# Decay attention and a two-layer MoE block on one core: low halves of all weights on VectorE, two more jobs in float32, decay rows by products, smaller first groups, and a planner with other costs

## The chip, the core and the metric

The kernel runs on one core of a Trainium2 chip. The core has five engines that run side by side, each in its own fixed order: TensorE (PE) for products, VectorE (DVE), ScalarE (ACT) and GpSimd (POOL) for element work, and SyncE (SP), whose queue issues all transfers. They wait for one another by semaphores. The metric is device time in microseconds (us); one execution was also recorded by the hardware profiler.

## What is computed

Eight batches of eight heads with 576 rows and 64 columns each: attention with a decay, then a feed-forward block over the 4608 rows of 512 columns that result.

```python
scores = scale * np.matmul(q, k.transpose(0, 1, 3, 2))
cum = np.cumsum(np.log(np.clip(f, 0.0001, 1.0)), axis=-1)
decay = cum[:, :, :, None] - cum[:, :, None, :]
scores = np.where(causal, -1000000000.0, scores + decay)
attn = softmax(scores)
x = np.matmul(attn, v)                  # to (4608, 512)
h = x @ w_in                            # (4608, 2048)
g = where(h >= 1, h, where(h <= -1, 0, (h + 1) ** 2 / 4))
out = g @ w_out                         # (4608, 512)
```

All inputs are float32. The kernel gets float32 accuracy from float16 products by splitting each factor into a high half and a low half (the rest), and adding three products: high by high, low by high, high by low. A product in float32 is the other way: one product, which PE takes in several passes.

## The kernel before

**Jobs.** Attention is cut into 36 jobs of two heads each (`jobs`). The first batch is cut in rows: jobs one to four do rows 0 to 255 of its eight heads, jobs five to eight rows 256 to 575; from job nine on, each job does all 576 rows of two heads. In the code jobs count from 0. A job goes row block by row block (128 rows, `r`): `scores` makes the products of q and k on PE and writes the decay term into a buffer (`sdr`, `sd4`) on POOL: a tensor_scalar on the broadcast row of cumulated logarithms, then an affine_select for the causal mask. `weights` adds scores and decay and takes the maximum on DVE, takes the exponential on ACT and the reciprocal of the sum on DVE.

**Two forms of a job.** Jobs with `w.p < NPE`, five of them before, stay in float32: `turn_rows` transposes the weights by products on PE with a diagonal matrix that holds the reciprocals (made on ACT), ACT copies the result to `pT`, and `early_values` multiplies it with float32 values. Later jobs split: ACT writes the high half, DVE (or POOL, where `POOL_LOW` says so: jobs seven and eight, row blocks 2 and 4) the low half, SP transposes both by transfers, and `values` makes three float16 products; `split_values` splits v on ACT and DVE. At the end of a job ACT and DVE evacuate its values to `x` as high and low halves. There is one `pT` buffer.

**Weights of the feed-forward block.** There are eight blocks of 256 hidden columns, each with a part of w_in and one of w_out: sixteen parts, loaded in float32 of which `weight_split` makes high and low halves in place. Three DVE instructions on 1024 words rearrange bits, ACT squares for a norm, a product on PE and small DVE instructions give a scale (`from_norms`), ACT writes the high half, and the low half is written by POOL for parts of w_in (a tensor_scalar, then a tensor_tensor) and by DVE for parts of w_out (one scalar_tensor_tensor). `CONVERT` says how many blocks are converted during which job.

**Feed-forward.** Tokens go in 18 chunks of 256. A unit is one chunk and one block: `moe_front` makes 24 products into a `ph` tile in PSUM (two such tiles, shared with the transposes), three ACT and two DVE instructions make `g` in halves, `moe_back` makes 12 products into `po`. A group of blocks shares its output scale, so that its units can start once all its blocks are converted; `EARLY` lists the groups of chunks 0 and 1. Chunk 0 needs jobs one to four, chunk 1 jobs five to eight, later chunks whole batches. `quota` spreads the ready units over the jobs.

**The order.** The program is recorded in the order of the code, and `plan` then sets an order for each engine: `arranged` is a list schedule over the recorded instructions with a cost for each (`Step.cost`), due ranks (place in the recording plus a shift by kind and engine, `SHIFT`), and models of PE's clock and of transfers. The engines run that fixed order.

Of the kernel before, what the change touches and what calls it, by code (L numbers as in the profile page):

```python
# [8 lines left out]
F32 = mybir.dt.float32  # L9
# [6 lines left out]
P = 128  # L16
# [14 lines left out]
NPE = 5  # L31
# [19 lines left out]
SLOW = 1.03  # L51
LOOK = 50
SHIFT = {
    ("from_norms", "PE"): -100,
    ("measure", "DVE"): 400,
    ("moe_back", "DVE"): 200,
    ("moe_back", "SP"): 800,
    ("split_values", "ACT"): 1500,
    ("turn_rows", "ACT"): -25,
    ("value_max", "DVE"): -100,  # L60
    ("weight_split", "DVE"): 200,
    ("weights", "POOL"): 400,
# [29 lines left out]
class Step:  # L92


    def __init__(self, k, ins):
        self.k, self.ins, self.engine = k, ins, ENGINES[ins.engine.name]
        self.reads, self.writes = ([self.part(a) for a in args if hasattr(a, "bass_ap")] for args in (ins.ins, ins.outs))
        self.after, self.waits, self.tiles = set(), [], set()

# [18 lines left out]
    def cost(self):  # L118
# [4 lines left out]
        if e == "PE":  # L123
            size, wide32 = self.ins.tile_size or (128, 128), self.reads[0][5] == 4
            half = 64 in tuple(size) and not self.ins.is_transpose
            t = n / 2.4 * ((2 if self.ins.is_transpose else 4) if wide32 else 1) * (0.5 if half else 1)
            return max(t + 3, 100 if wide32 else 28)
# [4 lines left out]
        if e == "ACT":  # L132
            return 150 + (0.82 if wide and wide[0][0][:2] in ("s_", "ph", "po") else 0.93) * n + 100 * min(len(self.reads) - 1 + len(self.writes) - 1, 3)
        if e == "POOL":
            if self.ins.opcode == "TensorTensor":
                return 450 + 2.0 * n
            return 260 + 0.95 * n if "Affine" in self.ins.opcode else 460 + 1.15 * n
# [3 lines left out]
        return 170 + 55 * (scalars > 0) + (0.6 if fast else 1.08) * n + (20 if len(self.writes) > 1 else 0)  # L141
# [67 lines left out]
def arranged(steps, users, order, rings):  # L209
# [16 lines left out]
    chains = {e: [] for e in LATE}  # L226
    fly, dma, warm, border, busy, form = [], 0.0, False, WINDOW, 0.0, None
# [3 lines left out]
    for _ in steps:  # L231
        best = None
        for e, cands in ready.items():
            pick = None
            for k, t in cands.items():
# [44 lines left out]
        elif e == "PE":  # L280
            work = s.time + (100 if form is not None and form != (64 in tuple(s.ins.tile_size or ())) else 0)
            form = 64 in tuple(s.ins.tile_size or ())
# [12 lines left out]
        else:  # L295
            end = t + s.time
            free[e] = end - OVERLAP[e]
# [23 lines left out]
def kernel(  # L321
# [138 lines left out]

    place = const.tile([P, 2 * NB + 1, 2, 2 * DM], F16, name="place")
# [25 lines left out]
    def weight_split(n0, n1):  # L487
# [77 lines left out]
    early_z = const.tile([P, 5, NB], F32, name="early_z")  # L565

    class Scales:
        pass

    @of_kind  # L570
    def moe_scales(b, first=0, last=NB - 1, early_group=False):
# [5 lines left out]
        w = early_z[:, :, blocks] if early_group else tiny.tile([P, 5, NB], F32, name="z")  # L577
        z.t, z.h, z.u, z.r, z.o = (w[:, i] for i in range(5))
        nc.vector.tensor_scalar(out=z.t, in0=sw[:, 0, blocks], scalar1=sv[:, b:b + 1], scalar2=None, op0=ALU.mult)
        nc.vector.tensor_scalar(  # L580
            out=z.h.bitcast(I32), in0=z.t.bitcast(I32), scalar1=1, scalar2=None, op0=ALU.logical_shift_right
        )
        nc.vector.tensor_scalar(
            out=z.h.bitcast(I32), in0=z.h.bitcast(I32), scalar1=HALF_BIAS, scalar2=None, op0=ALU.add
        )
        nc.vector.reciprocal(z.u, z.h)
        nc.vector.tensor_scalar(out=z.u, in0=z.u, scalar1=0.5, scalar2=None, op0=ALU.mult)
        nc.vector.tensor_scalar(out=z.h, in0=z.h, scalar1=0.5, scalar2=None, op0=ALU.mult)
# [633 lines left out]
```

## Time and profile before

| What | Value |
|---|---|
| median of 3 runs | 1060.62 us (1059.4 to 1061.3) |
| the profiled execution | 1060.71 us |
| its span, first to last instruction | 1058.9 us |
| mean granted TensorE clock, share of full | 0.973 |
| PE busy | 1003.1 us (95%) |
| DVE busy | 793.0 us (75%) |
| ACT busy | 786.9 us (74%) |
| POOL busy | 435.4 us (41%) |

Shares are of the whole span, and stages differ: attention and feed-forward work run together up to about 890 us, and feed-forward work alone after that. "Busy" counts an instruction from its start to its end, also where it is held up; "idle before" is time in which the engine had no instruction running, with the one that ended it. The TensorE clock has two levels, 1.2 and 2.4 GHz; the granted clock is the share of full speed.

### The profile page before, as it was taken

How to read it: one execution, taken by the hardware profiler on the slowest of the kernel's cores; microseconds unless marked ns; L12 is line 12 of the kernel's file. 1: busy time of each engine (PE TensorE's matmuls, PEld its weight loads, DVE VectorE, ACT ScalarE, POOL GpSimd, SP SyncE). 2: the span in 40 equal slices, each digit the busy share in tenths (PEclk: the TensorE clock that was granted, in tenths of full speed). 3: DMA queues.
4: the chain of work that ended last, by engine and by line, in shares of the span. 5: the costliest groups of instructions: out<-in, count | busy, mean ns of one | idle time of the engine just before them, and what ended most of it. 6: DMA issues, size and time to landing. Idle time of an engine off the chain costs nothing.

```text
span 1058.9 us, 24420 instructions
## 1 busy us (share of the span) xinstructions
PE 1003.1 (95%) x8859; PEld 657.7 (62%) x8859; DVE 793.0 (75%) x2095; ACT 786.9 (74%) x1634; POOL 435.4 (41%) x677
## 2 busy tenths in 40 slices
PE   3769888799999999999999999999999999999998
PEld 2546555366666676667666666666666666677665
DVE  5999999999998878977776677887788866322222
ACT  3788888788888878886776688888888877344443
POOL 2887776736443544442332344454445441000000
PEclk9869899889999999999999999999999999999999
DMA  9967669789997777785455476767676654000000
GB/s 298 305 203 206 167 163 194 182 169 187 198 189 184 175 167 151 170 185 128 119 128 131 81 175 144 158 150 160 147 161 143 142 104 95 3 22 19 3 20 20
DMA packets 406041, 152.18 MB, mean 144 GB/s; under 512 B 379680, under 2 KB 382752, under 8 KB 405920
## 3 DMA queue, kind: packets, MB, share of 16 engines
q1 hardware_dynamic: 405920, 150.62, 61.0%
q8 instruction: 69, 1.13, 0.5%
q14 instruction: 52, 0.43, 0.1%
HBM read 75.64 MB, written 9.58 MB: 80 GB/s over the span
## 4 chain that ended last, share of the span: by engine, by line
PE 56%; DMA 0%; DVE 0%; issue 0%; ACT 0%; DVEq 0%
PE ph L1012 25%; PE po L1041 24%; PE s L831 4%; PE s L968 3%; DMA vst<-in_v_dram 0%; DVE pr L947 0%; PE ph L409 0%; DVE u L1023 0%; PE ph L401 0%; DVE x L978 0%; ACT ot L1058 0%; PE ph L397 0%; ACT u L1022 0%; DVE sdr L923 0%; DVE rc L938 0%
## 5 line engine op out<-in xcount | busy, mean ns | idle before, releaser
L1012 PE MATMUL ph<-x,place 128*128 128x256 f16 (+3 forms) x4608 | 413.1, 247 | 1.2 <-DVE u L1023 0.7
L1041 PE MATMUL po<-place,g 128*128 128x512 f16 x1728 | 403.5, 381 | 2.3 <-ACT g L1025 1.0
L1012 PEld LDWEIGHTS <-place 128*128 128x128 f16 x4608 | 353.2, 99 | 61.9 <-issue 21.3
L1041 PEld LDWEIGHTS <-g 128*128 128x128 f16 x1728 | 165.9, 98 | 180.6 <-issue 8.0
L837 POOL TENSOR_SCALAR sdr<-ck,nsig,cqs 128x128 f32<-128x128 f32 (+1 forms) x192 | 150.1, 789 | 269.3 <-DVE pr L947 258.1
L1023 DVE SCALAR_TENSOR_TENSOR u<-ph,z,u 128x512 f32<-128x512 f32 x128 | 95.6, 747 | 128.5 <-ACT u L1022 128.3
L1021 ACT ACTIVATE u<-ph,z 128x512 f32<-128x512 f32 x128 | 98.8, 772 | 117.3 <-PE ph L1012 116.9
L927 ACT ACTIVATE sdr<-sdr,nm 128x384 f32<-128x384 f32 (+1 forms) x248 | 137.3, 555 | 24.7 <-DVE nm L923 22.2
L947 DVE SCALAR_TENSOR_TENSOR pr<-sdr,rc,pr 128x384 f16<-128x384 f32 (+2 forms) x232 | 126.7, 584 | 8.0 <-ACT pr L941 6.6
L1025 ACT ACTIVATE g<-u,z 128x512 f16<-128x512 f32 x128 | 91.8, 717 | 51.7 <-DVE u L1023 50.9
L1026 DVE SCALAR_TENSOR_TENSOR g<-u,z,g 128x512 f16<-128x512 f32 x128 | 98.2, 767 | 41.0 <-ACT g L1025 40.5
L941 ACT ACTIVATE pr<-sdr,rc 128x384 f16<-128x384 f32 (+1 forms) x236 | 118.7, 556 | 7.3 <-issue 2.8
L831 PE MATMUL s<-qkT 64*64 64x512 f16 (+11 forms) x1056 | 111.4, 336 | 6.0 <-DVE nm L923 2.9
L923 DVE CUSTOM_DVE_ANT_0 sdr<-s,sdr,nalpha 128x128 f32<-128x128 f32 (+1 forms) x192 | 99.0, 544 | 13.1 <-PE s L831 7.4
L841 POOL TENSOR_SCALAR_AFFINE_SELECT sdr<-sdr 128x128 f32<-128x128 f32 x248 | 97.7, 414 | 2.3
L837 POOL TENSOR_SCALAR sd<-ck,nsig,cqs 64x576 f32<-64x576 f32 x48 | 51.1, 1064 | 115.1 <-DMA ck<-cum_d 46.7
L1022 ACT ACTIVATE u<-u 128x512 f32<-128x512 f32 x144 | 89.7, 623 | 1.9
L968 PE MATMUL s<-pT,vs 128*64 128x320 f16 (+3 forms) x1098 | 69.8, 279 | 3.2 <-DVE nm L923 3.2
L968 PEld LDWEIGHTS <-vs 128*64 128x64 f16 x1098 | 48.6, 110 | 27.0 <-issue 9.3
L831 PEld LDWEIGHTS <-qkT 64*128 64x128 f16 (+1 forms) x864 | 32.4, 98 | 44.0 <-issue 29.4
L747 DVE SCALAR_TENSOR_TENSOR qs<-qk,sc,qs 128x640 f16<-128x640 f32 x48 | 45.6, 962 | 5.3 <-ACT qs L745 4.4
L837 POOL TENSOR_SCALAR sdr<-ck,cq 128x384 f32<-128x384 f32 (+3 forms) x48 | 40.4, 842 | 17.1 <-DVE pr L947 12.6
(157 smaller groups left out, 1027.7 us busy)
## 6 DMA issues: line engine op xcount, KB each, us to landing
ck<-cum_d SPq DMA_DIRECT2D x64, 288.0 KB, 4.0
out_dram<-ot SPq DMA_DIRECT2D x36, 256.0 KB, 2.2
qk<-in_k_dram SPq DMA_DIRECT2D x68, 128.0 KB, 2.7
vst<-in_v_dram SPq DMA_DIRECT2D x28, 288.0 KB, 3.4
v<-in_v_dram SPq DMA_DIRECT2D x62, 128.0 KB, 2.8
qk<-in_q_dram SPq DMA_DIRECT2D x60, 128.0 KB, 2.9
place<-in_moe_w_in_dram SPq DMA_DIRECT2D x6, 1024.0 KB, 6.9
place<-in_moe_w_out_dram SPq DMA_DIRECT2D x5, 1024.0 KB, 7.8
```

The costliest lines, as they stand in the source:

```text
L831: nc.tensor.matmul(sds[h % len(sds)][1][p0:p1, c0:c1], lhsT=a[rows, q0 - w.s0:q0 - w.s0 + p1 - p0], rhs=b[rows, c0:c1], start=(i == 0), st ...
L837: nc.gpsimd.tensor_scalar(out=sd[p0:p1, 0:wid], in0=w.ck[h][p0:p1, 0:wid], scalar1=w.nsig if w.p < NQK else w.nsig[p0:p1], scalar2=w.cqs[p ...
L841: nc.gpsimd.affine_select(sd[p0:p1, q0:wid], sd[p0:p1, q0:wid], pattern=[[-1, wid - q0]], channel_multiplier=1, base=0, compare_op=ALU.is_ ...
L923: nc.vector.tensor_tensor_reduce(out=a, in0=sp[:, 0:wid], in1=a, scale=w.nalpha, scalar=BIG, op0=ALU.add, op1=ALU.min, accum_out=nm[:, i:i ...
L927: nc.scalar.activation(a, a, AF.Exp, bias=nm[:, i:i + 1], scale=-1.0, accum_out=sm[:, i:i + 1])
L941: nc.scalar.activation(pr[:, :, 0, i, :], a, AF.Copy, scale=rc[:, i:i + 1])
L947: nc.vector.scalar_tensor_tensor(out=pr[:, :, 1, i, :], in0=a, scalar=rc[:, i:i + 1], in1=pr[:, :, 0, i, :], op0=ALU.mult, op1=ALU.subtract,)
L968: nc.tensor.matmul(av[64 * h:64 * h + 64, at + s0:at + s1], lhsT=w.vs[:, vl, h, t, :], rhs=w.pT[:, t, pl, h, s0:s1], start=(t == 0 and pi ...
L1012: nc.tensor.matmul(ph[:, fi, a0:a1], lhsT=wi[fb][:, wl, t, fi * P:(fi + 1) * P], rhs=xs[b][:, t, xl, s0:s0 + a1 - a0], start=(fi == 0 and ...
L1021: nc.scalar.activation(u, h, AF.Relu, scale=z.u[:, i:i + 1], bias=z.h[:, i:i + 1])
L1026: nc.vector.scalar_tensor_tensor(out=g[:, 1], in0=u, scalar=z.r[:, i:i + 1], in1=g[:, 0], op0=ALU.mult, op1=ALU.subtract)
L1041: nc.tensor.matmul(po[ch][i], lhsT=g[:, gl, fi * TC + i * P:fi * TC + (i + 1) * P], rhs=wo[fb][:, wl, fi, :], start=(first and fi == 0 and ...
```

## The change

- Low halves of all sixteen weight parts are made by DVE; the POOL pair of instructions is gone.
- `NPE` is 7: jobs six and seven (0-based 5 and 6) are float32 jobs as well.
- `NROW` is 2: for jobs one and two, the row of cumulated logarithms is spread over partitions by a float32 product on PE (with `picks`, copies of a column of the identity made on POOL) into a `po1` tile, and ACT forms the decay term from there; before, the row was written to DRAM and loaded 128 times, and POOL formed the term.
- Groups of chunk 0 are blocks 0-1, 2-3, 4-5, 6-7 (before 0-3, 4-5, 6-7), of chunk 1 0-5 and 6-7 (before 0-3, 4-5, 6-7). Scales of a block that an earlier group has made are not made again.
- `CONVERT` starts with job one, and one block a job; `FIRST` puts the values of job four ahead of the steps of job five, and two units behind its first step.
- The planner's costs, its margin (`SLOW`), its choice window (`LOOK`) and `SHIFT` change. It now has a rule that certain DVE instructions and POOL instructions hold one another up (`shares`, `hold`, `pool`), and it charges a change of PE tile shape for every pair of unequal shapes. No instruction comes from these; they move instructions in the engines' orders.

The constants and the lines that issue instructions:

```diff
-NPE = 5
+NPE = 7
+NROW = 2
...
-EARLY = ((0, 0, 4), (0, 4, 6), (1, 0, 4), (1, 4, 6), (0, 6, 8), (1, 6, 8))
-
-CONVERT = {1: 1, 2: 1, 3: 2, 5: 1, 6: 1, 9: 1, 10: 2}
+EARLY = ((0, 0, 2), (0, 2, 4), (0, 4, 6), (1, 0, 6), (0, 6, 8), (1, 6, 8))
+FIRST = {4: 2}
+
+CONVERT = {0: 1, 1: 1, 2: 1, 3: 1, 5: 1, 6: 1, 9: 1, 10: 2}
...
-SLOW = 1.03
-LOOK = 50
+SLOW = 1.02
+AWARE = True
+LOOK = 25
 SHIFT = {
+    ("decay_sums", "ACT"): 1500,
...
+                    if AWARE and s.shares:
+                        begin = max(begin, pool - 140)
+                    elif AWARE and e == "POOL":
+                        begin = max(begin, hold - 100)
...
-            work = s.time + (100 if form is not None and form != (64 in tuple(s.ins.tile_size or ())) else 0)
-            form = 64 in tuple(s.ins.tile_size or ())
+            shape = tuple(128 if d == 32 and i else d for i, d in enumerate(s.ins.tile_size or (128, 128)))
+            work = s.time + (94 if form is not None and form != shape else 0)
+            form = shape
...
-            if n % 2 == 0:
+            if False:
                 nc.gpsimd.tensor_scalar(out=word, in0=word, scalar1=s, scalar2=0.0, op0=ALU.mult, op1=ALU.add)
                 nc.gpsimd.tensor_tensor(out=lo, in0=word, in1=hi, op=ALU.subtract)
             else:
...
+        if w.p < NROW:
+            pt = ps1.tile([P, DM], F32, name="po1").rearrange("p (h s) -> p h s", h=2)
+            for h in range(2):
+                nc.gpsimd.tensor_copy(picks[h], ident[0:B * H, bh + h:bh + h + 1].broadcast_to([B * H, P]))
+                nc.tensor.matmul(
+                    pt[:, h], lhsT=picks[h], rhs=early[0:B * H, 2 * S:2 * S + w.s1], start=True, stop=True
+                )
+            w.ck += [pt[:, 0], pt[:, 1]]
+            picks[0:2] = []
+            return
...
+            if w.p < NROW:
+                nc.scalar.activation(
+                    sd[:, 0:wid], w.ck[h][:, 0:wid], AF.Identity, scale=w.nsig, bias=w.cqs[:, r, h:h + 1]
+                )
+            else:
...
-            steps.insert(4 if len(steps) == NT5 else 2, finish)
+            steps.insert(0 if p in FIRST else 4 if len(steps) == NT5 else 2, finish)
...
-        quota = -(-ready() // (NPAIR - (p + NPAIR - 1) % NPAIR))
+        quota = FIRST.get(p) or -(-ready() // (NPAIR - (p + NPAIR - 1) % NPAIR))
```

Three places of the orders. The first is ACT at the start. `qkT` are transposed inputs, `place` a weight part, `sdr` and `pr` the buffers of decay terms, `nm` the maxima. Before:

```order
L718 ACTIVATE qkT<-ph 128x2x256 x2
L505 ACTIVATE place,m2w<-place 128x1024 x2
L927 ACT_TABLE_LOAD
L927 ACTIVATE sdr_101,sm_227<-sdr_101,nm 128x128
L927 ACTIVATE sdr_102,sm_227<-sdr_102,nm 128x128
```

and now, where the rows from `po` are the new decay terms of jobs one and two:

```order
L784 ACTIVATE qkT<-ph 128x2x256
L904 ACTIVATE sdr_102<-po_143,cq 128x128
L904 ACTIVATE sdr_103<-po_143,cq 128x128
L904 ACTIVATE sdr_104<-po_143,cq 128x256
L904 ACTIVATE sdr_105<-po_143,cq 128x256
L904 ACTIVATE pr_112<-po_148,cq 128x128
L904 ACTIVATE pr_113<-po_148,cq 128x128
L904 ACTIVATE pr_114<-po_148,cq 128x256 x2
L784 ACTIVATE qkT<-ph 128x2x256
L998 ACT_TABLE_LOAD
L998 ACTIVATE sdr_102,sm_234<-sdr_102,nm 128x128
```

The decay terms of two jobs came ahead of the first exponential, and the squares of the first weight part went behind it.

The second is PE around the values of job four (their products are the rows that write `po`), up to the first product of the feed-forward block, the row with `x,place`. The rows `pr` are transposes of weights, the rows `qkT` scores, the rows `ident,qk` transposes of inputs. Before:

```order
L895 MATMUL po_710<-pT,vs 64x128
L409 MATMUL ph<-m2w,ones 128x2
L714 MATMUL s<-ident,qk_0_98 128x128 x2
L714 MATMUL s<-ident,qk_0_98 128x64
L863 MATMUL ph<-pr_110,sdr_101 128x128 x2
...
L831 MATMUL s<-qkT 128x384 x2
L831 MATMUL s<-qkT 128x512
L869 MATMUL ph<-pr_110,sd_0_105 128x128 x4
L869 MATMUL ph<-pr_110,sd_0_105 64x128
L831 MATMUL s<-qkT 128x512
L1012 LDWEIGHTS place
L1012 MATMUL ph<-x,place 128x256
```

and now:

```order
L897 MATMUL s<-qkT 64x512
L897 MATMUL s<-qkT 64x64 x2
L780 MATMUL s<-ident,qk_0_99 128x128
L966 MATMUL po_647<-pT,vs 64x256 x2
L966 MATMUL po_647<-pT,vs 64x128 x2
L1083 LDWEIGHTS place
L1083 MATMUL ph<-x,place 128x256
```

The products of the feed-forward block moved directly behind the values of job four, 48 of them in a row, and the transposes of job five behind those.

The third is POOL in the stretch with the first weight part's low half. The rows with `ck` or `ot` are decay terms, AFFINE_SELECT is the causal mask. Before:

```order
L837 TENSOR_SCALAR pr_113<-ot,cq 128x256 x2
L511 TENSOR_SCALAR place<-place,sw 128x1024
L841 AFFINE_SELECT pr_113<-pr_113 128x128
L512 TENSOR_TENSOR place<-place 128x1024
L841 AFFINE_SELECT pr_113<-pr_113 128x128
```

and now:

```order
L908 TENSOR_SCALAR pr_114<-ot,cq 128x256
L912 AFFINE_SELECT pr_114<-pr_114 128x128
L908 TENSOR_SCALAR pr_114<-ot,cq 128x256
L912 AFFINE_SELECT pr_114<-pr_114 128x128
L908 TENSOR_SCALAR sdr_102<-ck,cq 128x384
```

The two instructions on a weight part left, and each decay term is followed by its own mask.

## Rows read from the trace of the kernel before

**Rows 1.** The page's slices: PE's busy time and TensorE's granted clock in 40 equal slices of the span (26.5 us each), in tenths.

```profile
PE   3769888799999999999999999999999999999998
...
PEclk9869899889999999999999999999999999999999
```

**Rows 2.** Busy time of each engine by stretches of the span: us, PE busy (number of instructions), PE weight loads, DVE, ACT, POOL, granted clock, share of the DMA engines, GB/s.

```profile
0.00:30.00 30.00, 10.52 (x61) 7.52 (x61) 17.51 (x41) 10.94 (x25) 11.09 (x30) 1.00 0.91 302
30.00:66.00 36.00, 28.43 (x162) 19.63 (x162) 33.56 (x72) 28.20 (x68) 29.19 (x31) 0.72 0.77 228
66.00:86.00 20.00, 13.10 (x60) 9.35 (x60) 18.30 (x45) 15.42 (x36) 17.62 (x20) 0.74 0.95 321
86.00:120.00 34.00, 30.71 (x213) 18.46 (x213) 33.31 (x69) 30.65 (x58) 25.79 (x29) 0.90 0.64 152
120.00:200.00 80.00, 71.14 (x537) 42.38 (x535) 76.20 (x217) 69.36 (x149) 56.69 (x80) 1.00 0.78 179
200.00:230.00 30.00, 24.66 (x145) 12.86 (x147) 27.55 (x85) 23.38 (x51) 17.38 (x24) 0.72 0.79 184
230.00:1059.00 829.00, 824.52 (x7690) 547.50 (x7685) 586.59 (x1572) 609.00 (x1255) 277.67 (x468) 1.00 0.57 125
```

**Rows 3.** Instructions in order of time on DVE, then on POOL (two of the eight TENSOR_TENSORs that make low halves of weights): start us, duration us, engine, line, operation, out<-in, shapes, count.

```profile
41.20 2.09 DVE L514 SCALAR_TENSOR_TENSOR place<-place,sw 128x1024 f16<-128x1024 f32 x1
...
43.91 2.07 DVE L930 TENSOR_SCALAR rc<-sm 128x2 f32<-128x2 f32 x1
...
60.36 2.01 DVE L417 TENSOR_SCALAR mp<-mp 128x2 f32<-128x2 f32 x1
...
71.85 2.26 DVE L603 TENSOR_SCALAR early_z<-early_z 128x4 f32<-128x4 f32 x1
...
102.52 2.62 DVE L1026 SCALAR_TENSOR_TENSOR g<-u,early_z,g 128x512 f16<-128x512 f32 x1
...
200.22 2.09 DVE L583 TENSOR_SCALAR z<-z 128x8 int32<-128x8 int32 x1
...
43.42 2.54 POOL L512 TENSOR_TENSOR place<-place 128x1024 f16<-128x1024 f32 x1
...
60.22 2.13 POOL L512 TENSOR_TENSOR place<-place 128x1024 f16<-128x1024 f32 x1
```

**Rows 4.** Groups of DVE instructions of one line and shape, of the whole span (the second L1026 row: of the first 230 us alone), with count, busy us, mean ns of one; and two small instructions in order of time, undisturbed.

```profile
L1026 DVE SCALAR_TENSOR_TENSOR g<-u,z,g 128x512 f16<-128x512 f32 x128 | 98.2, 767 | 41.0 <-ACT g L1025 40.5
...
L947 DVE SCALAR_TENSOR_TENSOR pr<-sdr,rc,pr 128x512 f16<-128x512 f32 x62 | 44.8, 762 | 1.3 <-ACT pr L941 1.1
L947 DVE SCALAR_TENSOR_TENSOR pr<-sdr,rc,pr 128x384 f16<-128x384 f32 x58 | 35.0, 642 | 2.0 <-ACT pr L941 1.6
...
L795 DVE SCALAR_TENSOR_TENSOR vs<-v,sv,vs 128x640 f16<-128x640 f32 x31 | 28.2, 908 | 1.1 <-ACT vs L794 0.9
...
L947 DVE SCALAR_TENSOR_TENSOR pr<-sd,rc,pr 128x640 f16<-128x640 f32 x29 | 26.9, 929 | 1.3 <-ACT pr L941 1.3
...
L514 DVE SCALAR_TENSOR_TENSOR place<-x,sw,place 128x1024 f16<-128x1024 f32 x3 | 3.8, 1265 | 0.0
...
L1026 DVE SCALAR_TENSOR_TENSOR g<-u,early_z,g 128x512 f16<-128x512 f32 x12 | 14.6, 1213 | 0.0
...
195.28 0.17 DVE L586 RECIPROCAL early_z<-early_z 128x2 f32<-128x2 f32 x1
195.40 0.15 DVE L596 TENSOR_SCALAR gm<-gm 128x1 f32<-128x1 f32 x1
```

**Rows 5.** The start, in order of time on POOL, on DVE and on PE; in brackets the idle time just before an instruction and what ended it.

```profile
20.31 1.92 POOL L837 TENSOR_SCALAR sdr<-ot,cq 128x128 f32<-128x128 f32 x2 [17.24 <-DMA ot<-cum_d]
...
16.21 1.23 DVE L498 SCALAR_TENSOR_TENSOR qs<-place,qs 128x1024 int32<-128x1024 int32 x1
...
22.63 0.29 DVE L923 CUSTOM_DVE_ANT_0 sdr<-s,sdr 128x128 f32<-128x128 f32 x1 [0.63 <-POOL sdr L841]
...
25.47 0.17 DVE L930 TENSOR_SCALAR rc<-sm 128x2 f32<-128x2 f32 x1 [2.30 <-ACT sdr L927]
...
26.39 1.22 PE L863 MATMUL ph<-pr,sdr 128*128 128x128 f32 x4 [9.47 <-ACT pr L852]
...
34.22 0.87 PE L895 MATMUL po<-pT,vs 128*64 128x256 f32 x8
```

**Rows 6.** PE in order of time: eight float32 tiles (x16) transposed at a granted clock near half, five tiles (x10) of row 4, values of job five in float32 and of job six in float16.

```profile
76.51 3.78 PE L863 MATMUL ph<-pr,sdr 128*128 128x128 f32 x16 [2.52 <-ACT pr L852]
...
83.14 1.52 PE L869 MATMUL ph<-pr,sd 128*128 128x128 f32 x10
...
89.80 2.42 PE L895 MATMUL s<-pT,vs 128*64 128x320 f32 x20
...
104.58 1.75 PE L968 MATMUL s<-pT,vs 128*64 128x320 f16 x30
```

**Rows 7.** In order of time: on DVE the evacuations of the values of jobs four and twelve, on PE the first MoE product.

```profile
75.47 0.47 DVE L903 SCALAR_TENSOR_TENSOR x<-po,sv,x 128x256 f16<-128x256 f32 x1
...
85.65 0.39 PE L1012 MATMUL ph<-x,place 128*128 128x256 f16 x2
...
249.77 0.74 DVE L978 SCALAR_TENSOR_TENSOR x<-s,x 128x576 f16<-128x576 f32 x1
```

**Rows 8.** PE's waits in the first 230 us: who waited for whom, us in total, times, longest us.

```profile
PE ph L863 <- ACT pr L852: 22.7, 8, 9.5
```

More of the change, by code (lines that the diff above doesn't have):

```diff
@@ L50 @@
 RING = 1500
[L51 to L52 removed]
+SLOW = 1.02
+AWARE = True
+LOOK = 25
 SHIFT = {
+    ("decay_sums", "ACT"): 1500,
+    ("decay_sums", "SP"): -100,
+    ("first_values", "SP"): 200,
+    ("from_norms", "DVE"): -800,
     ("from_norms", "PE"): -100,
[L55 to L57 removed]
+    ("join_scales", "DVE"): -25,
+    ("load_first_decay", "PE"): 25,
+    ("load_first_decay", "POOL"): -100,
+    ("measure", "ACT"): -25,
+    ("measure", "DVE"): -25,
+    ("moe_back", "SP"): -800,
+    ("moe_front", "DVE"): 800,
+    ("moe_scales", "DVE"): 200,
+    ("prepare", "ACT"): 1500,
+    ("prepare", "DVE"): -1500,
+    ("prepare", "SP"): -200,
+    ("scores", "ACT"): 800,
     ("split_values", "ACT"): 1500,
[L59 to L62, printed above, removed]
+    ("value_max", "DVE"): -200,
+    ("values", "DVE"): -200,
+    ("weight_load", "SP"): 25,
+    ("weights", "POOL"): 200,
 }
@@ L98, in __init__ @@
         self.after, self.waits, self.tiles = set(), [], set()
+        self.shares = (
+            self.engine == "DVE" and ins.opcode in ("TensorScalarPtr", "TensorTensor")
+            and self.writes[0][4] > 1 and self.reads[0][0][:2] not in ("s_", "ph", "po")
+        )
     @staticmethod
@@ L296, in arranged @@
             end = t + s.time
+            if e == "POOL":
+                if hold > t:
+                    end = max(end, hold + s.time - 100)
+                pool = end
+            elif s.shares:
+                if pool > t:
+                    end = max(end, pool + max(s.time - 140, 24))
+                hold = end
             free[e] = end - OVERLAP[e]
@@ L457, in decay_sums @@
         )
+    picks = two.tile([P, 2 * TC], F32, name="u")
+    picks = [picks[0:B * H, P * i:P * i + P] for i in range(2 * NROW)]
     place = const.tile([P, 2 * NB + 1, 2, 2 * DM], F16, name="place")
@@ L576, in moe_scales @@
         n = last + 1 - first
[L577 to L588, printed above, removed]
+        if early_group:
+            at = groups.index((first, last + 1))
+            z.t, z.h, z.u = (early_z[:, i * NB + first:i * NB + first + n] for i in range(3))
+            z.r = early_r[:, starts[at]:starts[at] + n]
+            z.osc = early_r[:, starts[-1] + at:starts[-1] + at + 1]
+            fresh = slice(made[0], last + 1)
+            if made[0] <= last:
+                block_scales(*(early_z[:, i * NB + made[0]:i * NB + last + 1] for i in range(3)), b, fresh)
+                made[0] = last + 1
+        else:
+            w = tiny.tile([P, 5, NB], F32, name="z")
+            z.t, z.h, z.u, z.r = (w[:, i] for i in range(4))
+            z.osc = w[:, 4, 0:1]
+            block_scales(z.t, z.h, z.u, b, blocks)
         gm = tiny.tile([P, 1], F32, name="gm", bufs=2)
@@ L1180 @@
                 converted += 1
-            while ready() and done - before < quota * (i + 1) // len(steps):
+            while ready() and done - before < (quota if p in FIRST else quota * (i + 1) // len(steps)):
                 if units[done] not in bsc and nw < 2 * NB:
```

46 lines of the change are left out of this document (32 added, 14 removed).

## The prediction

> **What bounds the kernel now.** I read the page's slices first [rows 1]: PE (TensorE) is at 9 tenths or more in every slice from the ninth on, and the granted clock in every one from the tenth on; not before. The table by stretches [rows 2] makes that a sum. After 230 us PE is busy 824.5 of 829 us; what happens there on other engines costs nothing so long as PE is fed. Before 230 us it is not fed. I count as "wait" the idle time of a stretch plus busy time times the share of the clock that was not granted: 19.5 us (0 to 30), 7.6 + 8.0 (30 to 66), 6.9 + 3.4 (66 to 86), 3.3 + 3.1 (86 to 120), 8.9 (120 to 200), 5.3 + 6.9 (200 to 230). That is 45 us up to 86 and 27.5 from there to 230; 73 in all, beside 157 us of PE work at full clock. So the end is PE's work, some 982 us, plus its waits, 77. A change can win only what it takes from these 73 us, less what it adds to PE's work.
>
> What sets the pace there is the VectorE queue (DVE): busy 33.6 of 36, 18.3 of 20, 33.3 of 34, 76.2 of 80 us. Part of that is not work [rows 3]: at 43.91 a two-element TENSOR_SCALAR takes 2.07 us, where an undisturbed small one takes 0.15 [rows 4], while GpSimd (POOL) runs a 2.54 us TENSOR_TENSOR that makes a low half; 2.01 at 60.36, 2.26 at 71.85 and 2.09 at 200.22 lie on the same POOL operation (two of its runs are shown), and 2.62 at 102.52 is a form with a mean of 0.77. Of the start [rows 5]: POOL stands idle 17.24 us for the broadcast decay rows, the first row's maximum is at 22.63, the first transposing product at 26.39 after 9.47 us of idle PE.
>
> **The sum, part by part.** It is made against the profiled execution, 1060.71 us (span 1058.9), which is the median shown, 1060.62, to 0.1 us.
>
> (1) Jobs six and seven in float32 add PE work. Each adds 14 transposing products of a 128x128 tile for rows 2 and 3; eight took 3.78 us at a granted clock near half, so 0.24 us each at full clock, 3.3 us; five for row 4, 1.52 us; and its values take 2.42 in place of 1.75 us [rows 6]. That is 5.5 us a job, **+11**. The four broadcast products for jobs one and two (128x256 each, so two tiles' worth, 0.47 us) add **+1.9**, in PE's emptiest stretch. Work: +13.
>
> (2) Low halves on DVE, and what else its queue gains and loses. Eight more scalar_tensor_tensor of 1024 elements at 1.27 us undisturbed [rows 4]: +10.1. The float32 jobs drop two low halves of 384 elements, four of 512 and one of 640 (POOL made the others of job seven) and two value splits: 2 x 0.64 + 4 x 0.76 + 0.93 + 2 x 0.91 = -7.1. Two more groups of scales bring 24 small instructions, which start 0.12 us apart where they run undisturbed [rows 4], some closer: +2.4. DVE's work: +5. Against it stand the stalls: the five in rows 3 are worth 1.9 + 1.9 + 2.1 + 1.9 + 1.9, and POOL's eight pairs have others like them (twelve L1026 before 230 us average 1.21 us, 0.45 over their usual 0.77, 5.3 us in all, of which rows 3 show one). I put the stalls behind these pairs at 14 us, and what returns of them at 2. Net: DVE's path is 7 us shorter.
>
> By the Trainium skill, page SBUF — State Buffer, section Who interferes with whom, VectorE and GpSimd take a shared pair of ports as a lock held for a whole instruction; a VectorE instruction with two SBUF inputs contends with a GpSimd one that reads SBUF, and the second to issue blocks. That speaks against the move: the new low halves have two SBUF inputs, so the lock stays and only changes hands. The trace agrees with whole blocking (2.07 us for 0.16); that the new low halves block in their turn no row shows. By that rule the 2 us that return could be 8; this is the third rival.
>
> (3) Decay rows by products. The first decay tiles no longer wait for the 17.24 us, nor for POOL's 1.92 us. But the new DVE order puts the first two bit operations on a weight ahead of job one's first row, and these ended at 17.4 us [rows 5], since they wait for the weight's arrival. So the first row stands 5 us earlier (17.4 in place of 22.63), not 11, and the 2.30 us gap at 25.47 goes. I take 3 us of DVE idle time; bounds 0 and 7 (all idle time behind 15 us, and a part of what precedes it). The work that fills it is real: weights of the first block, one job earlier. The value loads of jobs one and two go behind the weight loads on SP's queue. With 10.4 MB ahead of them and 302 GB/s [rows 2] they land near 34.5 us, where job one's values ran before (34.22, rows 5). That costs nothing because the evacuation of job one now stands behind two more complete weight splits on DVE; without that cover each us of delay would hold the single buffer of weights (pT) and so job two.
>
> (4) Groups of two blocks. Before, the first MoE product is at 85.65, 10.2 us behind the evacuation of job four at 75.47 [rows 7]: it needs four blocks and their scales. In the new order 48 products follow directly on job four's values. That evacuation: 75.5, less 5.9 (three stalls of rows 3), less 0.8 (a low half lengthened at 41.20), less 3 of (3), plus 2.5 for two low halves that now stand ahead: 68. The first product there is 17.5 us earlier; of the 40 us of work before it, about 6 (transposes of job five, inputs of job six) now stand behind it, and 1.9 is new. Waits ahead of it: 45 before, 68 - 36 = 32 after, so -13 at best. The clock was near half at 70 to 80 us [rows 6], and 5.1 us of products at half clock cost up to 5 more; and DVE's added work (low halves, scales, the first units' element work) stands between 68 and 90 us, where PE then waits for it. I take **-9**, bounds -3 and -13.
>
> (5) 86 to 230 us. DVE's work is the same there within 2 us, and 7 to 8 us of stalls leave, so DVE's pace alone would shorten the stretch by 6 while PE has 11 us more to do: waits 27.5 - 17 = 10.5. Against that, PE runs in order, and float32 transposes wait for ACT's diagonal: 22.7 us in 8 waits in the jobs that have them now [rows 8]. If six more such groups wait like that, none of the 27.5 goes. Both ends are possible: **-9**, between 0 and -17, because MoE products stand between the transposes there, which those of the first jobs did not have.
>
> (6) After 230 us: the same products, and the changes of tile shape on PE are 197 in place of 201 over two thirds of the order. 0, within 2.
>
> Sum: 1060.7 + 13 - 9 - 9 = **1055.5 us**.
>
> **Rivals.** *A, slower: PE takes the place of DVE.* Mechanism: the 11 us of float32 work in jobs six and seven, and their waits for ACT's diagonals and for the two ph slots that MoE products need too, add to a stretch where PE is already busy 30.7 of 34 and 71.1 of 80 us. The waits of (5) stay: 1060.7 + 13 - 9 = 1065. For it: rows 8, and the busy shares. Against: DVE is fuller than PE in each of these stretches. It decides once less than 4 us of the 27.5 go.
>
> *B, both covers whole:* -13 and -17, so 1060.7 + 13 - 30 = 1044. For it: the stalls are the one thing in rows 3 without a reason to stay. Against: no stretch before 230 us has PE without waits now.
>
> *C, it does not do what it says: the lock moves with the low halves.* DVE or POOL blocks as before; stalls return at 8 rather than 2 us. Then (4) gives -7 and (5) -5: 1062. For it: POOL keeps its decay rows, most of its 29.2 of 36 and 56.7 of 80 us. Against: the longest stalls all lie on the 2.1 to 2.6 us TENSOR_TENSOR, and none so long on the 0.5 to 1 us decay operations.
>
> **How the numbers follow.** A measurement here tells 0.2% (2.1 us) from no change. Chances: forecast 0.50, A 0.22, B 0.18, C 0.10. The forecast's own range is 1049 to 1061, mostly below 1058.5; B is faster; A slower; C around no change. Faster 0.64, same 0.15, slower 0.21. The range reaches from B's 1044, with 3 us for the start's other bound, to A's 1065 with 2 us for (6): 1041 to 1067.
>
> **What would show it.** Right: first MoE product near 68 us; no DVE instruction of a few elements over 1 us; DVE's idle time in the first 30 us near 10 us (12.5 before); job twelve's evacuation, 249.77 now [rows 7], near 242; PE after 230 us as full as before. Wrong: if PE's first product is at 68 and the evacuation of job twelve still near 250, (5) failed and A holds, to be seen as PE waits on L863's successors in jobs six and seven; if short DVE instructions still take 2 us, C; if PE idles after 230 us, (6), which I priced at nothing, and the new order is the cause.

## The result, and the profile after

| | before | changed kernel |
|---|---|---|
| median | 1061.20 us (1059.40 to 1065.69, 6 runs) | 1068.12 us (1065.14 to 1072.43, 6 runs) |
| profiled execution | 1060.71 us, span 1058.9 | 1072.43 us, span 1070.7 |
| ratio | | 1.0067, 95% interval 1.0049 to 1.0085 |

The change makes the kernel slower by 0.7%; the forecast was 1055.5 us, and its range ended at 1067. The profiled execution of the changed kernel is the slowest of its six, so differences of traces below are some 5 us larger than those of medians.

The page of the changed kernel: PE's row of part 1, and the slices of PE and of the granted clock (26.8 us each), to be held against [rows 1].

```profile
PE 1023.2 (96%) x8923; PEld 673.4 (63%) x8923; DVE 763.4 (71%) x2118; ACT 788.0 (74%) x1649; POOL 396.5 (37%) x654
...
PE   6899998799999998999999999999999999999998
...
PEclk9969999999999999999999999999999999999999
```

PE starts earlier, as forecast: its first three slices read 6, 8, 9 in place of 3, 7, 6. What is new is a single 8 in the sixteenth slice (401 to 428 us), in the middle of a row of 9s. Slices hide such a thing; stretches show it. The same stretches as in [rows 2] (busy us of PE, PE weight loads, DVE, ACT and POOL with counts, granted clock, DMA share, GB/s):

```profile
0.00:30.00 30.00, 19.02 (x97) 14.66 (x97) 20.02 (x55) 16.41 (x43) 12.03 (x33) 1.00 0.96 322
30.00:66.00 36.00, 32.08 (x127) 20.03 (x128) 30.01 (x71) 28.52 (x64) 22.74 (x25) 0.79 0.86 215
66.00:86.00 20.00, 19.39 (x119) 13.44 (x119) 15.91 (x51) 14.79 (x31) 10.72 (x20) 0.86 0.96 304
86.00:120.00 34.00, 31.45 (x222) 21.22 (x219) 29.19 (x64) 28.06 (x63) 11.96 (x18) 1.00 0.45 118
120.00:200.00 80.00, 73.06 (x536) 42.32 (x533) 73.42 (x236) 70.02 (x150) 40.08 (x71) 1.00 0.86 183
200.00:230.00 30.00, 22.84 (x157) 14.17 (x159) 29.49 (x107) 23.33 (x50) 16.93 (x25) 0.89 0.77 161
...
230.00:1070.70 840.70, 825.40 (x7679) 547.56 (x7675) 565.39 (x1540) 606.89 (x1254) 282.02 (x466) 1.00 0.59 122
```

By the prediction's own account (wait = idle time plus busy time times the clock not granted) these rows give 44 us of waits ahead of 230 us, where [rows 2] give 73, and 15.3 us of idle PE behind 230 us, where they give 4.4. The rest of the span is PE's work: 1011 us in place of 982. So the waits ahead of 230 us fell by 29, more than the forecast 18; the work rose by 30, more than the forecast 13; and 11 us were lost where the prediction put nothing.

Where behind 230 us? One stretch holds nearly all of it, 10.3 us. First the row of the kernel before, then that of the changed kernel:

```profile
260.00:435.00 175.00, 175.00 (x1785) 116.32 (x1785) 154.30 (x449) 148.67 (x319) 82.06 (x139) 1.00 0.81 176
```

```profile
260.00:435.00 175.00, 164.69 (x1660) 109.50 (x1658) 136.59 (x402) 135.39 (x295) 74.39 (x122) 0.99 0.81 168
```

PE was busy 175.00 of 175 us and is now busy 164.69; DVE, too, did 18 us less there: it stood idle 38 us, where it had 21. What DVE stood for from 230 to 900 us, in the changed kernel (who waits for whom, us, times, longest):

```profile
DVE u L1094 <- ACT u L1093: 53.2, 39, 3.5
DVE m L582 <- DMA vst<-in_v_dram: 23.1, 8, 4.0
```

and the second of these in the kernel before:

```profile
DVE m L544 <- DMA vst<-in_v_dram: 6.2, 4, 2.5
```

The first row is the ordinary chain of an MoE unit. The second is the maximum of the next samples' values, which scales them: it needs a load into `vst`, a single buffer. In order of time, on SP, DVE and PE of the changed kernel (idle time just before, and what ended it, in brackets):

```profile
405.46 0.75 DVE L582 TENSOR_REDUCE m<-vst 128x1 f32<-128x576 f32 x1
405.57 0.93 SPq L708 DMA_DIRECT2D qk<-in_q_dram  x2
406.56 1.51 SPq L712 DMA_DIRECT2D qk<-in_q_dram  x1
...
408.17 1.09 SPq L708 DMA_DIRECT2D qk<-in_k_dram  x2
...
409.30 0.60 SPq L712 DMA_DIRECT2D qk<-in_k_dram  x1
...
410.00 0.54 SPq L575 DMA_DIRECT2D vst<-in_v_dram  x1
...
413.17 0.75 DVE L582 TENSOR_REDUCE m<-vst 128x1 f32<-128x576 f32 x1 [3.05 <-DMA vst<-in_v_dram]
...
414.37 0.61 DVE L994 CUSTOM_DVE_ANT_0 sdr<-s,sdr,nalpha 128x384 f32<-128x384 f32 x1
...
415.05 0.93 PE L897 MATMUL s<-qkT 64*64 64x512 f16 x12 [3.33 <-DVE nm L994]
```

The buffer was free at 406.2, but SP issued six loads for later jobs first and the value load at 410.0; it landed 3.1 us later; DVE stood 3.05 us; the row maxima behind it came late; and PE, which waits for the row maxima to get its score banks back, stood 3.33 us.

### The profile page after: what moved, and what is told of

It is laid out like the page before. It is cut to its first block, busy times and chain, and to the rows that moved or that the text cites. A ratio compares the mean times of both kernels' runs of the same rounds, so it can differ in the third digit from the quotient of the medians.

```text
span 1070.7 us, 24523 instructions
## 1 busy us (share of the span) xinstructions
PE 1023.2 (96%) x8923; PEld 673.4 (63%) x8923; DVE 763.4 (71%) x2118; ACT 788.0 (74%) x1649; POOL 396.5 (37%) x654
## 3 DMA queue, kind: packets, MB, share of 16 engines
q8 instruction: 70, 1.15, 0.4%
## 4 chain that ended last, share of the span: by engine, by line
PE 65%; SPq 3%; DVE 2%; DMA 2%; ACT 1%; issue 1%; DVEq 0%
PE ph L1083 28%; PE po L1112 27%; PE s L897 5%; PE s L1039 4%; DMA vst<-in_v_dram 2%; SPq L708 1%; SPq L712 1%; DVE sdr L994 0%; DVE pr L1018 0%; SPq L1027 0%; SPq L853 0%; DVE u L1094 0%; PE ph L445 0%; SPq L855 0%; ACT u L1092 0%
## 5 line engine op out<-in xcount | busy, mean ns | idle before, releaser
L908 POOL TENSOR_SCALAR sdr<-ck,nsig,cqs 128x128 f32<-128x128 f32 (+1 forms) x192 | 143.2, 749 | 271.1 <-DVE pr L1018 231.8
L1018 DVE SCALAR_TENSOR_TENSOR pr<-sdr,rc,pr 128x512 f16<-128x512 f32 (+1 forms) x226 | 124.1, 575 | 18.0 <-ACT pr L1012 16.5
L897 PE MATMUL s<-qkT 64*64 64x512 f16 (+11 forms) x1056 | 114.8, 333 | 5.7 <-DVE nm L994 5.4
L1012 ACT ACTIVATE pr<-sdr,rc 128x384 f16<-128x384 f32 (+1 forms) x228 | 114.0, 552 | 2.3 <-DVE rc L1006 0.9
L912 POOL TENSOR_SCALAR_AFFINE_SELECT sdr<-sdr 128x128 f32<-128x128 f32 x244 | 101.8, 429 | 16.8 <-ACT sdr L904 7.9
L908 POOL TENSOR_SCALAR sd<-ck,nsig,cqs 64x576 f32<-64x576 f32 x48 | 54.7, 1140 | 108.8 <-DMA ck<-cum_d 60.6
L1039 PE MATMUL s<-pT,vs 128*64 128x64 f16 (+4 forms) x1038 | 68.0, 283 | 2.8 <-DVE nm L994 2.0
L908 POOL TENSOR_SCALAR sdr<-ck,cq 128x384 f32<-128x384 f32 (+3 forms) x44 | 34.3, 780 | 54.0 <-DVE pr L1018 26.4
L811 ACT ACTIVATE qs<-qk,sc 128x640 f16<-128x640 f32 x48 | 39.0, 820 | 12.4 <-DVE sc L454 12.2
```

The source lines that it names most:

```text
L897: nc.tensor.matmul(sds[h % len(sds)][1][p0:p1, c0:c1], lhsT=a[rows, q0 - w.s0:q0 - w.s0 + p1 - p0], rhs=b[rows, c0:c1], start=(i == 0), st ...
L908: nc.gpsimd.tensor_scalar(out=sd[p0:p1, 0:wid], in0=w.ck[h][p0:p1, 0:wid], scalar1=w.nsig if w.p < NQK else w.nsig[p0:p1], scalar2=w.cqs[p ...
L912: nc.gpsimd.affine_select(sd[p0:p1, q0:wid], sd[p0:p1, q0:wid], pattern=[[-1, wid - q0]], channel_multiplier=1, base=0, compare_op=ALU.is_ ...
L1012: nc.scalar.activation(pr[:, :, 0, i, :], a, AF.Copy, scale=rc[:, i:i + 1])
L1018: nc.vector.scalar_tensor_tensor(out=pr[:, :, 1, i, :], in0=a, scalar=rc[:, i:i + 1], in1=pr[:, :, 0, i, :], op0=ALU.mult, op1=ALU.subtract,)
L1039: nc.tensor.matmul(av[64 * h:64 * h + 64, at + s0:at + s1], lhsT=w.vs[:, vl, h, t, :], rhs=w.pT[:, t, pl, h, s0:s1], start=(t == 0 and pi ...
```

## Experiments

"Work" and "waits" below are worked out from the same stretches as above, of the profiled execution of each run. The kernel before ran beside each, at medians of 1060.6 to 1060.7 us; the ratios are to it.

**1. The value loads ahead of the run of loads, all else held.** After the planner is done, the last twelve value loads are moved on SP's queue:

```diff
+def ahead(chain):
+    out, loads = [], 0
+    for s in chain:
+        at = len(out)
+        loads += s.writes[0][0].startswith("vst")
+        if s.writes[0][0].startswith("vst") and loads > 16:
+            while out[at - 1].writes[0][0].startswith(("qk32", "v32", "ck")):
+                at -= 1
+            if out[at - 1].writes[0][0].startswith("vst"):
+                at = len(out)
+        out.insert(at, s)
+    return out
...
     chains = arranged(*traced(nc, rings, kinds), rings)
+    chains["SP"] = ahead(chains["SP"])
```

> The changed kernel with one thing moved: of the last twelve value loads (vst, for the value maxima behind 230 us) each that stands behind a run of q, k, v and decay loads on SP's queue is put ahead of that run; every other instruction stands where it stood, on all engines. Theory (the loss arises behind 230 us: DVE takes the value maxima early and stands for loads that SP issues late, and PE then waits for DVE): DVE's wait for vst behind 230 us falls from 23.1 us to under 6, PE's gaps behind 230 us from about 11 us to under 5, and the time from 1068 to about 1061, 1058 to 1063. Rival 1 (the loss is the 13 us of float32 products): the waits for vst fall, and the time stays at 1068 within 1. Rival 2 (DVE stands there for other things that then come last): the wait moves to another releaser, 1065 to 1068.

Measured: 1058.80 us (1054.64 to 1061.74, 12 runs), ratio 0.9975 (0.9963 to 0.9988): 9.3 us less than the changed kernel, by nothing but the place of some loads, and faster than the kernel before. DVE's wait and PE's stretch in its trace (its lines are 15 further down):

```profile
DVE m L597 <- DMA vst<-in_v_dram: 9.5, 5, 2.9
```

```profile
260.00:435.00 175.00, 172.32 (x1743) 114.89 (x1743) 146.86 (x429) 143.63 (x311) 83.09 (x135) 1.00 0.88 176
```

PE's idle time behind 230 us goes from 15.3 to 7.3 us (waits ahead of 230 us: 45, as before the edit; work 1004). The wait did not fall as far as I expected (9.5, not under 6), the time further. Rivals 1 and 2 of this run fall: the float32 work is all still there, and no other row of DVE's waits there grew by more than 3.5 us, while PE's idle time fell by 8.

**2. The planner's number for the value maximum set back.**

```diff
-    ("value_max", "DVE"): -200,
+    ("value_max", "DVE"): -100,
```

> The changed kernel with the planner's number for value_max on DVE back at -100 (it is -200), everything else as it is; the planner then makes a new order for all engines. Theory: the value maxima are spread to about 520 us as before the change, DVE's wait for vst behind 230 us is under 10 us, and the time is 1060 to 1064. Rival 1 (float32 products): 1068 within 2. Rival 2 (other numbers of the planner, those of moe_back and prepare on SP or moe_front on DVE): the waits for vst fall, but other waits of PE behind 230 us take their place, 1066 or more.

Measured: 1075.26 us (6 runs), 1.0134 (1.0112 to 1.0156). A miss: DVE still stood 18.2 us for `vst` behind 230 us, PE 14.5 us, and the new order was worse elsewhere too (waits ahead of 230 us 48). One number of the table moves all engines, and setting this one back did not take the wait away, so it is not shown to be what made it. From here on, a new order by itself is to be reckoned with at some 7 us; run 12 shows 16.

**3 and 4. The change with the old planner; the new planner alone.** The planner's prices, rules and table (SLOW, LOOK, SHIFT, AWARE, `cost`, `arranged`) are exchanged between the two kernels.

> The whole change of what is computed where (float32 jobs six and seven, low halves on DVE, decay rows by products, groups of two blocks), but with the planner of before: its prices, its look ahead, its table of numbers, no rule for the lock. Theory (the new order loses behind 230 us, the new structure wins ahead of it): PE's gaps behind 230 us under 3 us, first MoE product within 10 us of 68, time 1054 to 1062. Rival 1 (the structure loses, by the float32 products): 1065 or more, with PE as full behind 230 us as before. The old numbers were not made for this structure, so the start may also come out worse, which the place of the first MoE product will show.

> The kernel before with the planner of the change alone: new prices, lock rule, table of numbers; what is computed where is as before. Theory: the value maxima come early as in the changed kernel, DVE waits for vst behind 230 us by 10 us or more, PE has gaps there of 5 us or more, and the time is 1064 to 1070, slower than before. Rival 1 (the structure is what loses): 1058 to 1061, PE as full behind 230 us as before.

Measured: the change with the old planner 1070.75 us, 1.0099 (1.0083 to 1.0115); the planner alone 1092.65 us, 1.0308 (1.0287 to 1.0329). The first is a miss in time: its first MoE product is at 72.9, but PE's idle time behind 230 us is 10.9, and its order, too, lets DVE stand for `vst` (14.1 us in 8 waits), so that wait does not need the new table. The second is slower, but far more than expected, and not for the reason given: behind 230 us DVE stands only 5.1 us for `vst`, yet PE stands idle 16.1 us, 11.9 of it in two waits for row maxima, and the waits ahead of 230 us are 82, where they were 73. Either half alone is slower than the kernel before; that a table fits only the structure it was made for would explain it, but is not shown. What both halves tell is in the waits of the transposing products for ACT's diagonals, over the span, first of the planner alone, then of the change with the old planner:

```profile
PE ph L897 <- ACT pr L886: 21.9, 6, 14.2
```

```profile
PE ph L900 <- ACT pr L889: 2.2, 3, 1.7
```

The wait of [rows 8] (22.7 us) goes with the structure, whichever planner is used.

**5 to 8. One part undone, with the value loads ahead as in 1.** Each gets a new order, with a table that was not made for it, so none of these times is the price of the part alone: by run 12 a new order alone can cost 16 us.

```diff
-NPE = 7
+NPE = 5
```

> The kernel of the run with the value loads ahead (1058.8 us), with jobs six and seven not in float32 (NPE 5); the planner makes a new order for it with the numbers of the change, and those were not made for it: a renumbering alone has cost some 7 us. So it is read by the account as well: PE's work is busy time by stretch times granted clock, the rest of the span is wait. With the value loads ahead: work 1002.5, wait 54. Step (1) of the prediction (11 us of work for these two jobs): work near 991. What the traces suggest now (the float32 products of these jobs cost some 15, since transposing products take 0.28 to 0.33 us and not 0.24): work near 987. Waits: if taking these jobs off DVE is what shortened them ahead of 230 us, they rise by 10 or more and the time is 1058 to 1066; if not, they stay near 54 and the time falls to about 1045.

Measured: 1065.73 us, 1.0055 (1.0037 to 1.0073); work 990, waits ahead of 230 us 68 in place of 45. So the order with the float32 products of jobs six and seven has some 15 us more of PE's work and 23 us less of waits; how much of the 23 is due to the new order is not shown.

```diff
-            if False:
+            if n % 2 == 0:
```

> The kernel with the value loads ahead, with the low halves of the even weights on POOL again (two POOL instructions each, as before the change), newly ordered by the planner of the change, which now knows the lock. Step (2) of the prediction (DVE's path 7 us longer, stalls of some 14 us back): short DVE instructions of 1 to 2 us return, waits ahead of 230 us rise by 5 to 10, time 1064 to 1070. Rival C (who makes the low halves does not matter, the lock goes with them): 1057 to 1061 with the stalls unchanged. Third reading (the planner's lock rule is what keeps the stalls away, as the planner alone already had few): no stalls return and yet POOL's pairs stand in the way of its decay rows, 1060 to 1068.

Measured: 1065.33 us, 1.0043 (1.0025 to 1.0061). Lengthened instructions are back, though the planner knows the lock; a low half and a small one on DVE, in order of time, then POOL's TENSOR_TENSORs that they lie on:

```profile
105.02 3.04 DVE L567 SCALAR_TENSOR_TENSOR place<-place,sw 128x1024 f16<-128x1024 f32 x1
...
124.67 2.10 DVE L673 TENSOR_TENSOR early_z<-early_z,sw 128x2 f32<-128x2 f32 x1
...
104.84 2.13 POOL L565 TENSOR_TENSOR place<-place 128x1024 f16<-128x1024 f32 x1
...
124.62 2.13 POOL L565 TENSOR_TENSOR place<-place 128x1024 f16<-128x1024 f32 x1
```

Undisturbed, a low half takes 1.27 us. The time is 6.5 us above run 1, as expected, but a new order alone can make as much, so the price is not shown. The waits ahead of 230 us rose by 19 us, not 5 to 10; 14 of that is clock not granted.

```diff
-NROW = 2
+NROW = 0
```

> The kernel with the value loads ahead, with the decay rows of jobs one and two loaded by DMA again (NROW 0), newly ordered. Step (3): the broadcast products' work leaves (3.8 us of PE busy time in the trace, priced at 1.9), DVE's idle time in the first 30 us rises by 3 to 7, and the first row's maximum goes from 18 to 21 to 23 us; time 1059 to 1065. Rival (the start has slack and the products are only work): 1055 to 1057.

Measured: 1074.63 us, 1.0152 (1.0116 to 1.0187), a far larger effect than I expected: 16 us more than with the products. Its trace, in order of time on POOL and PE, PE's wait over the first 230 us, and the decay rows' loads in the first 30 us (KB each, median us to landing):

```profile
21.39 0.88 POOL L923 TENSOR_SCALAR sdr<-ot,cq 128x128 f32<-128x128 f32 x1 [18.32 <-DVE place L554]
...
28.89 1.22 PE L949 MATMUL ph<-pr,sdr 128*128 128x128 f32 x4 [12.64 <-ACT pr L938]
```

```profile
PE ph L949 <- ACT pr L938: 23.3, 5, 12.6
```

```profile
ot<-cum_d SPq DMA_DIRECT2D x4, 256.0 KB, 10.8
```

The releaser named in the first row is not the cause: POOL's first decay row reads `ot`, whose loads landed 10.8 us after their issue, the first of them issued at 10.40; in [rows 5], too, POOL waited for them. PE's chain of the first jobs starts late, and waits add up in the next two jobs too (PE stands idle 18.6 and 13.7 us in the first two stretches, 11.0 and 5.6 with the products). DVE's idle time in the first 30 us, which I had expected to rise, is 9.6 us, 10.1 with the products.

```diff
-EARLY = ((0, 0, 2), (0, 2, 4), (0, 4, 6), (1, 0, 6), (0, 6, 8), (1, 6, 8))
-FIRST = {4: 2}
+EARLY = ((0, 0, 4), (0, 4, 6), (1, 0, 4), (1, 4, 6), (0, 6, 8), (1, 6, 8))
+FIRST = {}
```

> The kernel with the value loads ahead, with the MoE groups and the table of first units of before (0 to 4, 4 to 6, 6 to 8, no units taken early for job five), the table of weight splits per job as changed; newly ordered. Step (4): the first MoE product goes from 68 us to 78 to 87, PE waits ahead of it rise by 9, between 3 and 13; time 1062 to 1072. Rival (DVE's pace decides ahead of 230 us, and PE's early products only move its idle time): first product late, time 1057 to 1061.

Measured: 1058.74 us, 0.9983 (0.9972 to 0.9994), the same as with groups of two, with the first MoE product 24 us later:

```profile
87.88 2.78 PE L1098 MATMUL ph<-x,place 128*128 128x256 f16 x24
```

Its waits ahead of 230 us are 39, 45 in run 1. The rival holds: no gain by early MoE products shows here, nor between runs 9 and 11 below.

**9 to 12. Variants of the mended kernel.** Nine: without `and loads > 16`, so all 28 value loads are moved. Eleven: that, with the groups of run 8. Ten and twelve, each by one edit (ten on the changed kernel, twelve on that of run 1):

```diff
-            end = max(dma, t + s.time) + (2700 if s.reads[0][0].startswith("cum_d") else 1900)
+            end = max(dma, t + s.time) + (2700 if s.reads[0][0].startswith("cum_d") else 3900 if s.writes[0][0].startswith("vst") else 1900)
...
-AWARE = True
+AWARE = False
```

> As the run with the value loads ahead, but all 28 value loads are moved ahead of the runs of loads in front of them, those ahead of 230 us too, where DVE still stands 6.2 us in 4 waits for vst. Theory (DVE sets the pace ahead of 230 us, so its waits are time): those waits fall under 3 us, time 1053 to 1057 where the last twelve alone give 1058.8. Rival (a value load put ahead delays q, k and value loads that are needed sooner there): 1059 to 1063.

> The changed kernel with one number of the planner changed: it takes 3.9 us in place of 1.9 us from a value load's issue to its landing (the trace: median 3.2, up to 5.5), and makes its own order. Theory (the planner puts a value maximum where it believes the load landed, and DVE stands for the difference): DVE's wait for vst over the span falls from 29.7 us to under 10, PE's gaps behind 230 us halve, time 1056 to 1063. Rival (a new order costs more than the wait, as with value_max at -100): the waits for vst fall and the time is 1065 to 1075.

> All value loads ahead, and groups of four as before the change (that run gave 1058.7 with the last twelve ahead). If both hold alone: groups of four no loss, all loads ahead a gain, time 1053 to 1057; if groups of two use the early loads, 1057 to 1061.

> The kernel with the last twelve value loads ahead, low halves on DVE as changed, but the planner's rule for the lock off (AWARE False), so newly ordered. If taking the pairs off POOL is what ends the stalls (step (2)): DVE's lengthened instructions ahead of 210 us stay near 7 us in all, and the time is 1056 to 1063. If the planner's rule keeps them away: they go to 12 us or more, time 1063 to 1072.

Measured: nine 1059.63 us, 0.9985 (0.9972 to 0.9998), a miss, with no gain over the last twelve alone; the early waits for `vst` shrink only from 6.2 to 4.8 us, so the theory about them was not tried by it. Behind 230 us they shrink from 9.5 to 1.7 us and PE's idle time only from 7.3 to 6.5, so what run 1 left of them cost PE little. Ten 1059.71 us, 0.9991 (0.9978 to 1.0003): the wait is gone over the whole span,

```profile
DVE m L582 <- DMA vst<-in_v_dram: 3.1, 2, 1.8
```

PE's idle time behind 230 us is 7.1, and the whole loss of the change is gone with one number of the planner and the order that it makes. Eleven 1056.45 us, 0.9958 (0.9944 to 0.9972): the best version, faster than both kernels. Its time was expected, but not for the reason given, since run 9 shows no gain by the early loads alone; why it is faster than run 8 is open. Twelve 1075.30 us, 1.0135 (1.0115 to 1.0155), above both ranges. It has no DVE instruction of up to eight elements over 0.85 us ahead of 230 us, so moving the low halves is enough against the stalls; but its order makes PE wait behind 230 us, which I had not expected:

```profile
PE s L912 <- DVE nm L1009: 9.5, 5, 4.6
```

A count over all DVE instructions ahead of 230 us tells the same. Take those that ran at least 0.3 us longer than the lower quartile of their operation and shape over all runs, and add up the excess: 22 us before and 4 in the changed kernel; 4 in run 3 and 6 in run 12, both without the lock rule; 8.5 in run 4 and 13 in run 6, which have the rule but keep half of the low halves on POOL.

## Why the prediction was wrong, step by step

**(6), after 230 us: 0, within 2. This step failed**, and with it the sign. I counted the products and the changes of tile shape there, found them the same, and took PE's fullness for granted, although the diff changed the order of all engines. In the new order the last value maximum on DVE stands at 413 us, where it stood at 520; the planner believes, as the old one did, that a load lands 1.9 us after its issue, and `vst` took longer, by the view of that tile:

```profile
DMA to landing us min/median/max: 2.7/3.2/5.5
```

It took no less before (median 3.4 us); what changed is how close the maxima stand to their loads. DVE stood for them eight times behind 230 us, 23.1 us in all. Run 1 (place of the loads, all else held) takes 9.3 us back, with 8.0 of the 10.9 us of PE's new idle time, so this cause is shown, not argued; run 10 (the landing time alone, with the new order that it makes) agrees with 8.4. Not shown is which number of the planner packed the maxima (runs 2 and 3), nor where the last 2.9 us of idle time come from. The prediction's last sentence named the sign ("if PE idles after 230 us, (6)") but gave it no chance and no price.

**(1), +13 of work.** Mis-sized: by the account +30 in the profiled execution, +23 in run 1. The transposing products cost more than the eight tiles of [rows 6] suggest; the changed kernel's in a stretch at full clock, 86 to 200 us, and the broadcast products, of the whole span (two records for each float32 product; busy us, mean ns):

```profile
L934 PE MATMUL ph<-pr,sdr 128*128 128x128 f32 x28 | 3.7, 278 | 0.0
...
L934 PE MATMUL ph<-pr,pr 128*128 128x128 f32 x22 | 3.4, 287 | 1.8 <-ACT pr L923 1.8
...
L934 PE MATMUL ph<-pr 128*128 128x128 f32 x6 | 1.2, 286 | 0.0
```

```profile
L722 PE MATMUL po<-x,u 64*128 64x256 f32 x8 | 4.1, 664 | 0.0
```

That is 8.3 us for 28 products, 0.30 us each, where I took 0.24 (half of a time at half clock), although the five tiles of row 4 in [rows 6], at a granted clock of 1.00, already showed 0.30; and 4.1 us where I took 1.9 for the broadcast. With the 15 us of run 5 that makes 19 of the 23 of run 1. The rest of the 30 is not settled: PE's busy time rose by 20.1 us, by 13.1 in run 1, and busy time lost to the clock fell by 9, which the account turns into work.

**(2), low halves on DVE: -7.** The mechanism held. Before, seven DVE instructions of up to eight elements took 0.92 us or more ahead of 230 us, four of them in [rows 3]; now there is one:

```profile
133.82 1.29 DVE L659 TENSOR_SCALAR early_z<-early_z 128x2 f32<-128x2 f32 x1
```

By the count above, which takes in every cause, DVE's instructions lost 22 us and now lose 4, where I put the stalls at 14 and 2; what that is worth in the kernel's time no run shows by itself. The Trainium skill's page SBUF — State Buffer, section Who interferes with whom, gave the lock, and the blocked instructions of run 6 agree with it. So does an instruction of POOL: the lock did move with the low halves, as rival C said, but here POOL waits, and the stalls of DVE did not return. In the changed kernel a causal mask took 1.15 us beside a low half on DVE, and 0.29 soon after:

```profile
31.99 1.39 DVE L552 SCALAR_TENSOR_TENSOR place<-place,sw 128x1024 f16<-128x1024 f32 x1
...
32.39 1.15 POOL L912 TENSOR_SCALAR_AFFINE_SELECT pr<-pr 128x128 f32<-128x128 f32 x1
...
35.10 0.29 POOL L912 TENSOR_SCALAR_AFFINE_SELECT pr<-pr 128x128 f32<-128x128 f32 x1
```

**(3), decay rows by products: 3 us, at most 7.** Far too small. DVE's idle time in the first 30 us fell to 10 us as forecast, but it was the wrong thing to price: in run 7, with loaded rows and a new order, it is no longer, and yet the time is 16 us more. I put the 22.7 us of [rows 8], whose longest wait stands in [rows 5], under (5) as what float32 jobs bring with them. They go with the loaded, late decay rows: with these they are 22.7 (before), 21.9 (run 4) and 23.3 (run 7), with products 2.2 to 6.6 in all other runs, whatever the order. In the changed kernel:

```profile
PE ph L934 <- ACT pr L923: 5.8, 4, 2.8
```

**(4), groups of two: -9.** The event came as forecast, the gain did not. The evacuation of job four and the first MoE product, on DVE and on PE:

```profile
68.83 0.48 DVE L974 SCALAR_TENSOR_TENSOR x<-po,sv,x 128x256 f16<-128x256 f32 x1 [0.81 <-ACT x L973]
```

```profile
68.21 4.03 PE L1083 MATMUL ph<-x,place 128*128 128x256 f16 x20
```

68 was forecast for both, against [rows 7]. But run 8 is as fast with the first product at 87.9; that PE has other work to fill that time is the likely reason, not a shown one.

**(5), 86 to 230 us: -9.** Waits there went from 27.5 to 19 us (2.6, 6.9 and 9.7 in the last three stretches), -8; job twelve's evacuation is at 244.7 (242 forecast). Rival A, slower because PE takes the bound, got the sign but not the mechanism: the waits that it counted on fell.

So what (2) to (5) did to the waits ahead of 230 us was worth 29 us, not 18; (1) took that back; and (6) decided. Without (6)'s loss the kernel runs at 1058.8, inside the forecast's own range, but with luck: by run 1 the work was 10 us more than forecast, and the waits fell by 10 us more. (The parts of the sum add up to 1055.7, not 1055.5.)

## What to carry to other kernels

When a change makes a new order, "the same instructions" is no reason for a cost of nothing in a stretch where the bound engine is full: ask which wait the new order brings nearest to its data, and check the planner's latency for that transfer against the landing times in the trace. A load into a single buffer that the pace-setting chain waits for is worth moving ahead of the prefetches in front of it on its queue: here that gave 9 us for the last twelve loads, and nothing more for the earlier ones. And a wait is to be put to the event that starts its chain, not to the engine named in the row: the 22.7 us for ACT's diagonals went with decay rows that came late at the start. Last, a part is not priced by undoing it and planning anew: here a new order alone moved the time by up to 16 us.

## What was not expected of the hardware

The same order does not give the same clock: the changed kernel and that of run 1 have one order up to 230 us, and their granted clock in the five stretches from 30 us on was 0.79, 0.86, 1.00, 1.00, 0.89 and 0.81, 1.00, 0.95, 0.97, 0.91, in one execution each.

A float32 transposing product does not take exactly twice as long at half clock. In the changed kernel from 52 to 71 us:

```profile
52.00:71.00 19.00, 19.00 (x66) 10.03 (x63) 13.72 (x48) 12.28 (x29) 11.08 (x16) 0.50 0.93 255
```

```profile
L934 PE MATMUL ph<-pr,pr 128*128 128x128 f32 x12 | 3.3, 448 | 0.0
```

That is 0.45 us a record, where 86 to 200 us, at full clock, show 0.28: 1.6 times as long; by busy time (3.3 us for 12 records, 8.3 for 56) 1.9 times. So an account that splits PE's time into work and clock, as the prediction's and mine here, is good to a few us only.
